# Attention beside a routed feed-forward: the lead of row maxima in groups of three pairs, V's last tile in another bank, one output tile finished by VectorE

## The chip, the cores and the metric

One core of a Trainium2 chip runs the whole program. Its engines work side by side, each through its own queue in program order: TensorE (PE, with the weight loads, PEld, as a second row of the profile), VectorE (DVE), ScalarE (ACT), GpSimd (POOL) and the queue of SyncE (SP), from which most DMAs are issued. They meet at semaphores. PE writes to PSUM, which has eight banks of 128 partitions x 512 float32; DVE and ACT read it, POOL doesn't. The metric is the device time of one execution in microseconds (us), the median of several; lower is better.

## The reference

x is 2048 x 512 (S x D), there are 32 heads of 16 columns, and everything is float32:

```python
g = sigmoid((x * gate_w).sum(-1, keepdims=True))
q, k, v = split_heads(x @ wqkv)
p = softmax(einsum("bhqd,bhkd->bhqk", q, k) * 16 ** -0.5)
a = merge_heads(einsum("bhqk,bhkd->bhqd", p, v)) @ wo
r = x @ w_r
idx = argsort(-r)[:, :2]
y = (silu(x[idx] @ w_gate) * (x[idx] @ w_up)) @ w_down * sigmoid(r[idx])
b = x + scatter_add(0, idx, y)
out = g * a + (1 - g) * b
```

## The kernel before

**Units.** Heads are taken two at a time (a pair of heads sits in rows 0 to 47 and 64 to 111 of `Qx` and `Kx`: high parts, low parts and a copy of 16 columns each). A pair of heads and one half of the queries is a unit; there are 32, and each has 16 steps, one for each 128 keys. Unit 0 uses `Kx[0]` and `Qx[0]`.

**What a unit needs first.** Softmax subtracts each row's maximum. `m_piece` and, ahead of the main loop, `m_lead` compute the scores with queries on the partitions (t: eight blocks of 128 queries; c: four blocks of 512 keys; j: the head of the pair) and reduce them on DVE to `Mr`, one column for each (t, c, j): 64 columns a unit (`EL`). `m_unit` takes the minimum over c of the negated maxima, `m_rows` transposes it and writes it by eight small DMAs on SP into rows 48 and 49 (and 112 and 113) of `Qx`, where it takes part in the second score matmul, `s_piece`. That one has the keys on the partitions; ACT takes its exp into `P`, and `av_mm` multiplies P with V (with a column of ones for the sums) into a bank that is collected over a unit's 16 steps.

**PSUM.** The eight banks have fixed names: `st` three in rotation, `mxa` two banks as one tile of 1024 columns, and one each of `mxb`, `av` and `fl`. A tile of a name waits until the engines have read what was in the same bank before (three allocations back for `st`, one for the others).

**The start.** Q and K of the first group of heads are projected, then comes the lead: `LEAD` = 21 steps, numbered -21 to -1. Each step calls `m_lead(n)`, which issues two pairs of matmuls (one pair into `mxa`, the second into two of `mxb`, `fl`, `av` in turn, both with the same t and neighbouring c) and three reductions on DVE; then three parts (four in the first step) of `lead_parts`; then the work filed for that step. A part is three matmuls on all 128 rows: the first four parts are the last projection of Q, the other 64 are V, four for each tile of 128 tokens (`v_part`). A V tile is collected in an `st` bank and copied to SBUF by ACT (L303) with its last part. 21 steps take 64 of the 68 parts; the last four, V's tile 15, are left to the main loop. `m_unit(0)` follows n = 15, `m_rows` of unit 0 n = 16.

**Work filed for steps** (`at_step`, run by `end_step`): `products(t)` at step -18 + t, two POOL multiplications of a block of x with w_r and gate_w; `sums(t)` at -17 + t, two ACT passes that add them up into `gz`; loads of x at -13 and -9; W of the second group of heads loaded at -8 and split at -5 (`split_w(1)`: high parts by ACT, low parts by POOL); `r_row` at -1, a PE transpose of `gz` into `fl`, copied by ACT when the main loop runs its list `late`. The products' tiles come from a ring of six, of which four are free for them, so products t wait for sums t - 2.

**The main loop** runs through the string `ORDER`, each letter of which issues one thing: `s` a score matmul with its exp, `m` one matmul of the maxima (with a reduction after the second and the third of each three), `A` P V of one step, `f` a filler (three matmuls of a later projection, in `fl`). The first two `A` come before P V has data: each takes two parts of V instead (L1025). The segments of the string are called rounds' segments below: "sssmmA", "smssmmA", "msssmmf", "smssmmA", and so on.

**The tail** (L796 to L848) multiplies the last unit's output with `wo` and stores the last output tiles of 128 tokens. A tile is brought to its end either by `finish`, one DVE instruction that reads PSUM, or by `acc_add`, an ACT copy with the gate's scale and a POOL addition. Tiles 10, 11, 12, 14 and 15 are finished by DVE, 9 and 13 by `acc_add`. The stores of 10, 11, 9, 12, 14 and 13 stand in this order on SP's queue; tile 15's two halves are stored from ACT's queue.

Of the kernel before, what the change touches and what calls it, by code (L numbers as in the profile page):

```python
# [21 lines left out]
KT = S // 128  # L22
VW = DH + 1
LEAD = 21
# [12 lines left out]
def gated_mix(ctx: ExitStack, tc: tile.TileContext, xT, x, wqkv, wo, w_rg, w_gate, w_up, w_down,  # L37
# [12 lines left out]
    def st_tile(shape=(128, 512)):  # L50
        return psum.tile(list(shape), F32, tag="st", name="st", bufs=3)
# [4 lines left out]
    def mxa_tile():  # L56
        return psum.tile([128, 2, 512], F32, tag="mxa", name="mxa", bufs=1)
# [4 lines left out]
    def av_tile():  # L62
        return psum.tile([128, 512], F32, tag="av", name="av", bufs=1)
# [229 lines left out]

    def v_part(t, c):
        if c == 0:
            VP[t] = st_tile()
        ps = VP[t]
        nb, tt = divmod(t, 4)
        sl = slice(tt * 128, tt * 128 + 128)
        for n, (a, b) in enumerate(((xh, wv[1]), (xl, wv[1]), (xh, wv[2]))):  # L300
            nc.tensor.matmul(ps, a[nb][:, c, sl], b[:, c, :], start=c == 0 and n == 0, stop=c == 3 and n == 2)  # L301
        if c == 3:
            nc.scalar.activation(Vh[:, t, :, :DH], ps.rearrange("p (h d) -> p h d", d=DH), AF.Copy)  # L303

    def lead_parts():

        v = [(t, c) for t in range(KT) for c in range(4)]
        yield from proj(0, "q", 3, 3)
        while v:
            v_part(*v.pop(0))  # L310
            yield


    rg = {}
# [27 lines left out]
    def r_row():  # L342
        ps = fl_tile((16, 128))
        nc.tensor.transpose(ps, gz[:, :, 0], ident)
        rg["row"] = ring.tile([16, 128], F32, tag="rt", name="rt", bufs=1)
        late.append((nc.scalar.activation, (rg["row"], ps, AF.Copy)))

    def route_rows():

# [124 lines left out]
    def acc_add(t, ps, scale):  # L474
        a = acc[t // 4][:, t % 4, :]
        w = o_tile("w", [128, D])
        nc.scalar.activation(w, ps, AF.Copy, scale=scale[:, t:t + 1])  # L477
        nc.gpsimd.tensor_add(a, a, w)  # L478
# [132 lines left out]

    def m_lead(n):

        if n < 16:
            u, t, c = 0, n // 8 * 4 + n % 4, n // 4 % 2 * 2
        else:
            u, t, c = 1, (n - 16) // 2, n % 2 * 2
        for i in range(3):
            if i == 0:
                tl = mxa_tile()  # L620
                dst = [tl[:, 0], tl[:, 1]]
            else:
                tl = (mxb_tile, fl_tile, av_tile)[(2 * n + i) % 3]()
                dst = [tl]
            for k, d in enumerate(dst):
                j, cc = (k, c) if i == 0 else (i - 1, c + 1)
                nc.tensor.matmul(d, Qx[u][64 * j:64 * j + 48, t * 128:t * 128 + 128],  # L627
                                 Kx[0][64 * j:64 * j + 48, cc * 512:cc * 512 + 512], start=True, stop=True)
            o = EL * u + t * 8 + (c * 2 if i == 0 else c * 2 + 1 + i)
            reds.append((Mr[:, o:o + len(dst)], tl))  # L630
        for r in reds:
            nc.vector.tensor_reduce(*r, axis=AX.X, op=OP.max, negate=True)  # L632
        reds.clear()
        if n == 15:
            m_unit(0)
        elif n == 16:
            m_rows(*turn.pop())

    reds = []
# [156 lines left out]
    def tail():  # L796
        u = UNITS - 1
        hl = [o_tile(n, [128, 512], F32R) for n in ("onh", "onl")]
        o = AV[u]
        ps = st_tile((128, 16))  # L800
        pw = mxa_tile()
        pw = pw[:, 0], pw[:, 1], st_tile()

        def late_wo(i):
            wo_terms(pw[i], *lastp[1], 3, slice((2 + i if i < 2 else 1) * 128, (3 + i if i < 2 else 2) * 128), True, True)

        late_wo(0)
        finish(10, pw[0])
        store(10)
        for c in range(4):  # L810
            nc.tensor.matmul(ps[:, 4 * c:4 * c + 4], o[:, c * 128:c * 128 + 128], sel_l, start=True, stop=True)
        r = ring.tile([128, 16], F32, tag="r16", name="rl", bufs=2)
        nc.vector.reciprocal(r, ps)
        rx = o_tile("rxl", [128, 16, 32])
        rb = r[:, :, None].to_broadcast([128, 16, 32])
        nc.scalar.activation(rx[:, 0:8], rb[:, 0:8], AF.Copy)
        nc.vector.tensor_copy(rx[:, 8:16], rb[:, 8:16])
        late_wo(1)
        finish(11, pw[1])
        store(11)  # L820
        pr = [mxb_tile((128, 256)), fl_tile((128, 256))]
        for c in range(4):
            nc.tensor.matmul(pr[c // 2][:, c % 2 * 128:c % 2 * 128 + 128],
                             rx[:, 4 * c:4 * c + 4].rearrange("p a b -> p (a b)"), ident, start=True, stop=True)
        for t in range(2):
            nc.vector.tensor_mul(o[:, 256 * t:256 * t + 256], o[:, 256 * t:256 * t + 256], pr[t])
        for t in range(2):
            sl = slice(256 * t, 256 * t + 256)
            split(hl[0][:, sl], hl[1][:, sl], o[:, sl])
        late_wo(2)  # L830
        acc_add(9, pw[2], gg)
        store(9)
        banks = [st_tile(), av_tile(), st_tile(), mxb_tile()]
        for t, n in ((0, 0), (0, 1), (1, 0), (1, 1), (0, 2), (1, 2), (2, 0), (2, 1), (2, 2), (3, 0), (3, 1), (3, 2)):
            a, b = ((0, 0), (0, 1), (1, 0))[n]
            nc.tensor.matmul(banks[t], hl[a][:, t * 128:t * 128 + 128], wz[0][:, b, :], start=n == 0, stop=n == 2)
            if n == 2 and t < 3:
                if t == 1:
                    acc_add(13, banks[t], gg)
                else:  # L840
                    finish(12 + t, banks[t])
                    store(12 + t)
        store(13)
        a = acc[3][:, 3, :]
        for i, eng in enumerate((nc.scalar, nc.scalar)):
            c = slice(256 * i, 256 * i + 256)
            nc.vector.scalar_tensor_tensor(a[:, c], banks[3][:, c], gg[:, 15:16], a[:, c], op0=OP.mult, op1=OP.add)
            eng.dma_start(out[15 * 128:, c], a[:, c])  # L848
# [4 lines left out]
    def at_step(s, f, *a):  # L853
        fill.setdefault(s, []).append((f, a))

    def end_step(s):
        now[0] = s
        for f, a in fill.pop(s, []):
            f(*a)
# [4 lines left out]
        at_step(-17 + t, sums, t)  # L864
    for t in range(16):
        at_step(-18 + t, products, t)
    at_step(-1, r_row)
    at_step(2, gaps.append, lambda: nc.vector.max(top8, rg["row"]))
    at_step(3, gaps.append, route_rows)
    at_step(1, gates, 0)  # L870
# [119 lines left out]
    def parts_next(n):  # L990
        for _ in range(n):
            next(parts, None)
# [4 lines left out]
            for c in (2 * nb - 4, 2 * nb - 3):  # L997
                split(wv[1][:, c], wv[2][:, c], wvs[:, c], lo_engine=nc.gpsimd)
    nc.sync.dma_start(cst, consts)
    for s in range(-LEAD, 0):  # L1000
        now[0] = s
        if s == -11:
            load_q(1)
        m_lead(s + LEAD)
        parts_next(3 + (s == -LEAD))
        end_step(s)
    count["m"] = 4 * LEAD

    while count["m"] < UNITS * EL:
# [71 lines left out]
```

## Time and profile before

| | us |
|---|---|
| median of 3 runs | 1415.55 (1415.53 to 1415.92) |
| the profiled execution | 1415.73 |
| its span, first to last instruction | 1413.8 |
| granted clock of TensorE | 1.000 |
| lead, first pair of maxima to the first score matmul of the main loop | 25.22 to 87.80 |
| last P V ends | 1401.4 |

The span is 1.93 us shorter than the execution's own time. A timeline row reads: start and duration in us, engine, line of the kernel, operation, output tile <- inputs, shapes, count, and in brackets how long the engine had been idle and what released it. A row of stretches reads: from and to, length, then the busy time of PE, PEld, DVE, ACT and POOL with their instruction counts, the granted clock, the share of time in which the DMA engines were busy, and GB/s. Durations of matmuls are modelled and overlap; starts are what to go by. Durations of DVE and ACT instructions overlap their neighbours by up to a tenth of a microsecond too.

### The profile page before, as it was taken

The numbers are of one execution on the slowest core, as the hardware profiler recorded it, in microseconds if no ns is written. First come the engines' busy times: TensorE is split into PE (matmuls) and PEld (weight loads), VectorE is DVE, ScalarE is ACT, GpSimd is POOL, SyncE is SP. The second block draws the span as 40 slices with busy tenths as digits, with TensorE's granted clock in tenths as the row PEclk, the third lists the DMA queues.
The fourth block names the chain that finished last, engine by engine and source line by source line (L and its number), as shares of the span: only waits on it lengthen the run. The fifth ranks groups of instructions, "written<-read, shape, count | busy, mean of one in ns | idle before, by whom it ended". The sixth has DMA issues, their size and how long they took to land.

```text
span 1413.8 us, 24075 instructions
## 1 busy us (share of the span) xinstructions
PE 1405.9 (99%) x9109; PEld 626.4 (44%) x9109; DVE 1287.5 (91%) x1535; ACT 1169.9 (83%) x2263; POOL 316.7 (22%) x335
## 2 busy tenths in 40 slices
PE   9999999999999999999999999999999999999998
PEld 6654444444444444444444443344444444444433
DVE  6889999999999999999999999999999999999943
ACT  5568888888888888888888888888888888888986
POOL 3841101102000001200000100043722322224411
PEclk9999999999999999999999999999999999999999
DMA  8712111312123221312222342424312121111002
GB/s 265 272 31 57 46 40 39 84 39 69 44 74 101 70 61 39 83 38 72 66 91 61 93 102 76 103 60 120 84 46 54 32 68 29 29 31 51 15 32 99
DMA packets 54775, 101.24 MB, mean 72 GB/s; under 512 B 13168, under 2 KB 20592, under 8 KB 53028
## 3 DMA queue, kind: packets, MB, share of 16 engines
q1 hardware_dynamic: 53796, 98.62, 24.6%
q8 instruction: 72, 1.18, 0.4%
q10 hardware_dynamic: 576, 0.79, 0.2%
q0 software_dynamic: 288, 0.30, 0.1%
q14 instruction: 43, 0.35, 0.1%
HBM read 63.77 MB, written 36.96 MB: 71 GB/s over the span
## 4 chain that ended last, share of the span: by engine, by line
PE 99%; DMA 0%; ACT 0%; DVE 0%; issue 0%; DVEq 0%
PE av L695 36%; PE st L672 23%; PE mxa L592 12%; PE mxb L592 10%; PE fl L155 6%; PE fl L511 4%; PE st L301 3%; PE st L155 2%; PE mxa L627 1%; PE fl L402 1%; PE mxa L672 0%; PE fl L440 0%; DMA ws<-wqkv 0%; PE mxa L511 0%; PE fl L627 0%; PE mxb L627 0%
## 5 line engine op out<-in xcount | busy, mean ns | idle before, releaser
L674 ACT ACTIVATE P<-st 128x512 f32<-128x512 f32 x2009 | 1055.3, 599 | 188.5 <-PE st L672 101.7
L596 DVE TENSOR_REDUCE Mr<-mxa 128x2 f32<-128x1024 f32 x655 | 796.1, 1215 | 2.6 <-PE mxa L592 2.5
L695 PE MATMUL av<-P,V 128*32 128x512 f32 x4096 | 545.6, 605 | 0.2 <-DVE o L704 0.2
L672 PE MATMUL st<-Qx,Kx 50*128 50x512 f32 x2009 | 531.4, 443 | 0.8 <-ACT P L674 0.6
L596 DVE TENSOR_REDUCE Mr<-mxb 128x1 f32<-128x512 f32 x654 | 451.0, 690 | 61.0 <-PE st L672 18.8
L672 PEld LDWEIGHTS st<-Qx,Kx 50*128 50x128 f32 x2009 | 276.5, 184 | 228.3 <-ACT P L674 208.7
L592 PE MATMUL mxb<-Kx,Qx 48*128 48x512 f32 x654 | 325.2, 497 | 0.0
L592 PE MATMUL mxa<-Kx,Qx 48*128 48x512 f32 x1310 | 294.1, 417 | 0.0
L592 PEld LDWEIGHTS mxb<-Kx,Qx 48*128 48x128 f32 x654 | 119.5, 183 | 273.7 <-DVE Mr L596 272.8
L695 PEld LDWEIGHTS av<-P,V 128*32 128x32 f32 x4096 | 81.1, 108 | 142.7 <-issue 135.9
L592 PEld LDWEIGHTS mxa<-Kx,Qx 48*128 48x128 f32 x1310 | 123.1, 183 | 44.3 <-DVE Mr L596 2.6
L208 POOL TENSOR_SCALAR ev<-pe 128x512 fp32r<-128x512 f32 x24 | 35.8, 1490 | 411.5 <-ACT pe L206 411.5
L478 POOL TENSOR_TENSOR acc<-acc,w 128x512 f32<-128x512 f32 x36 | 46.1, 1280 | 201.0 <-ACT w L477 200.9
L77 POOL TENSOR_SCALAR hl<-m 128x16 fp32r<-128x16 f32 x31 | 7.8, 253 | 296.5 <-DVE m L643 296.5
L155 PE MATMUL fl<-xh,wh 128*128 128x512 f32 x96 | 42.9, 447 | 0.0
L155 PE MATMUL fl<-xh,wl 128*128 128x512 f32 x96 | 40.5, 422 | 0.0
L511 PE MATMUL fl<-woh,ahl 128*128 128x512 f32 x96 | 35.1, 447 | 0.0
L562 DVE SCALAR_TENSOR_TENSOR acc<-fl,gg,acc 128x512 f32<-128x512 f32 x11 | 8.2, 747 | 28.8 <-PE fl L511 28.8
L632 DVE TENSOR_REDUCE Mr<-mxa 128x2 f32<-128x1024 f32 x21 | 25.7, 1222 | 8.5 <-PE mxa L627 8.5
L155 PE MATMUL fl<-xl,wh 128*128 128x512 f32 x96 | 32.6, 421 | 0.0
L303 ACT ACTIVATE V<-st 128x512 f32<-128x512 f32 x16 | 9.6, 600 | 27.5 <-PE st L301 27.5
L209 POOL TENSOR_TENSOR ev<-pe,ev 128x512 fp32r<-128x512 f32 x24 | 30.8, 1285 | 2.0
(192 smaller groups left out, 786.4 us busy)
## 6 DMA issues: line engine op xcount, KB each, us to landing
Kx<-k_scr SPq DMA_DIRECT2D x30, 384.0 KB
Qx<-q_scr SPq DMA_DIRECT2D x52, 192.0 KB
q_scr<-ev SPq DMA_DIRECT2D x15, 512.0 KB
k_scr<-ev SPq DMA_DIRECT2D x13, 512.0 KB
xn<-x SPq DMA_DIRECT2D x4, 1024.0 KB
Qx<-hr SPq DMA_DIRECT2D x256, 2.0 KB
acc<-x_scr SPq DMA_DIRECT2D x4, 1024.0 KB
q_scr<-ev SPq DMA_DIRECT2D x15, 256.0 KB
```

Source lines behind the costliest of these rows:

```text
L155: nc.tensor.matmul(ps, a[:, i, c, :], b[nb][:, c, :], start=n == 0, stop=n == 11)
L208: nc.gpsimd.tensor_scalar(ev[:, 0], t, 1.0, None, op0=OP.mult)
L209: nc.gpsimd.tensor_sub(ev[:, 1], t, ev[:, 0].bitcast(F32))
L301: nc.tensor.matmul(ps, a[nb][:, c, sl], b[:, c, :], start=c == 0 and n == 0, stop=c == 3 and n == 2)
L478: nc.gpsimd.tensor_add(a, a, w)
L511: nc.tensor.matmul(ps, a[:, sl], b[:a.shape[0], c, :], start=first and n == 0, stop=last and n == 2)
L592: nc.tensor.matmul(dst, Qx[u % 3][64 * j:64 * j + 48, t * 128:t * 128 + 128], k_of(u, t // 4)[64 * j:64 * j + 48, c * 512:c * 512 + 512], ...
L596: nc.vector.tensor_reduce(Mr[:, g0:g0 + (2 if r == 1 else 1)], MX[r - 1], axis=AX.X, op=OP.max, negate=True)
L632: nc.vector.tensor_reduce(*r, axis=AX.X, op=OP.max, negate=True)
L672: nc.tensor.matmul(ps, k, q, start=True, stop=True)
L674: nc.scalar.activation(P[s][:, 2 * j + c, :], ps, AF.Exp)
L695: nc.tensor.matmul(AV[0][32 * ct:32 * ct + 32, :], V[:, kt, h * VW:h * VW + 32], P[s][:, ct, :], start=kt == 0, stop=kt == KT - 1)
```

## The change

Three edits, with what follows from them:

1. `m_lead` runs 14 times and issues three pairs each time: the first into `mxa`, the second into an `st` and the `av` bank, the third into `mxb` and `fl`. A pair has one (t, c) and both heads. DVE reduces the double bank with one instruction and the other four banks with one each. After a group come five parts, or four in every third group (n = 1, 4, 7, 10, 13), 65 in all, and then the filed work of one or two steps, so that 14 groups cover the same 21 steps. `m_unit(0)` follows group 10, `m_rows` of unit 0 group 11, `load_q(1)` comes before group 6.
2. V's tile 15 is collected in the `av` bank. Its first part lies in the lead, the other three in the main loop. `r_row` is no longer filed for step -1: it is the last of the parts, right behind V's tile 15, and ACT's copy follows it at once rather than from the list `late`.
3. In the tail, tile 9 is brought to its end by `finish` (one DVE instruction), not by `acc_add` (ACT and POOL).

```diff
     def v_part(t, c):
         if c == 0:
-            VP[t] = st_tile()
+            VP[t] = av_tile() if t == KT - 1 else st_tile()
...
         while v:
             v_part(*v.pop(0))
             yield
+        r_row()
+        yield
...
-        late.append((nc.scalar.activation, (rg["row"], ps, AF.Copy)))
+        nc.scalar.activation(rg["row"], ps, AF.Copy)
...
     def m_lead(n):
 
-        if n < 16:
-            u, t, c = 0, n // 8 * 4 + n % 4, n // 4 % 2 * 2
-        else:
-            u, t, c = 1, (n - 16) // 2, n % 2 * 2
         for i in range(3):
+            p = 3 * n + i
+            if p < 32:
+                u, t, c = 0, p // 16 * 4 + p // 2 % 4, p // 8 % 2 * 2 + p % 2
+            else:
+                u, t, c = 1, (p - 32) // 4, p % 4
             if i == 0:
-                tl = mxa_tile()
-                dst = [tl[:, 0], tl[:, 1]]
+                tl = [mxa_tile()]
+                dst = [tl[0][:, 0], tl[0][:, 1]]
             else:
-                tl = (mxb_tile, fl_tile, av_tile)[(2 * n + i) % 3]()
-                dst = [tl]
-            for k, d in enumerate(dst):
-                j, cc = (k, c) if i == 0 else (i - 1, c + 1)
+                dst = tl = [st_tile(), av_tile()] if i == 1 else [mxb_tile(), fl_tile()]
+            for j, d in enumerate(dst):
                 nc.tensor.matmul(d, Qx[u][64 * j:64 * j + 48, t * 128:t * 128 + 128],
-                                 Kx[0][64 * j:64 * j + 48, cc * 512:cc * 512 + 512], start=True, stop=True)
-            o = EL * u + t * 8 + (c * 2 if i == 0 else c * 2 + 1 + i)
-            reds.append((Mr[:, o:o + len(dst)], tl))
+                                 Kx[0][64 * j:64 * j + 48, c * 512:c * 512 + 512], start=True, stop=True)
+            o = EL * u + t * 8 + c * 2
+            w = 2 // len(tl)
+            for j, k in enumerate(tl):
+                reds.append((Mr[:, o + j:o + j + w], k))
...
-        if n == 15:
+        if n == 10:
             m_unit(0)
-        elif n == 16:
+        elif n == 11:
             m_rows(*turn.pop())
...
         late_wo(2)
-        acc_add(9, pw[2], gg)
+        finish(9, pw[2])
         store(9)
...
-    at_step(-1, r_row)
...
-    for s in range(-LEAD, 0):
-        now[0] = s
-        if s == -11:
+    for n in range(LEAD * 2 // 3):
+        now[0] = n * 3 // 2 - LEAD
+        if n == 6:
             load_q(1)
-        m_lead(s + LEAD)
-        parts_next(3 + (s == -LEAD))
-        end_step(s)
+        m_lead(n)
+        parts_next(4 if n % 3 == 1 else 5)
+        for s in range(n * 3 // 2, (n + 1) * 3 // 2):
+            end_step(s - LEAD)
```

## The prediction

> **What bounds the kernel now.** I read the page, then the busy time of each engine in the lead, then the timelines of TensorE (PE), ScalarE (ACT), GpSimd (POOL) and VectorE (DVE) at the places that the diff touches: the lead (25 to 88 us), the first three rounds of the main loop, and the last 10 us. The page, and the lead's row (us; then busy us and instructions of each engine, granted clock, DMA share, GB/s):
>
> ```profile
> span 1413.8 us, 24075 instructions
> ...
> PE 1405.9 (99%) x9109; PEld 626.4 (44%) x9109; DVE 1287.5 (91%) x1535; ACT 1169.9 (83%) x2263; POOL 316.7 (22%) x335
> ...
> 25.00:91.00 66.00, 65.85 (x292) 42.88 (x291) 53.62 (x70) 32.82 (x87) 44.40 (x37) 1.00 0.56 187
> ```
>
> PE is the bound, in the lead too, so a change pays what it takes off PE's own sequence, plus what it takes off the end behind PE. "Busy" hides how densely PE works; that is read from start to start. One group of the lead (start, duration):
>
> ```profile
> 34.89 0.50 PE L627 MATMUL mxa<-Kx,Qx 48*128 48x512 f32 x2
> ...
> 35.23 0.39 PE L627 MATMUL av<-Kx,Qx 48*128 48x512 f32 x1
> ...
> 35.56 0.50 PE L301 MATMUL st<-Kx,xh 128*128 128x512 f32 x1
> 35.89 0.40 PE L301 MATMUL st<-Kx,xl 128*128 128x512 f32 x1
> ...
> 37.50 0.39 PE L301 MATMUL st<-wvl,xh 128*128 128x512 f32 x1
> ...
> 37.82 0.50 PE L627 MATMUL mxa<-Kx,Qx 48*128 48x512 f32 x2
> ```
>
> The two matmuls of a pair use different rows of the array and run side by side. Pair 1 to pair 2: 0.34 us. Pair 2 to the first V matmul: 0.33. First to second V: 0.33. Then V costs 0.23 each (35.89 to 37.50 in 7). Last V to the next pair: 0.32. A group of 2 pairs and 9 V matmuls is 2.93 us, of which 9 x 0.23 = 2.07 is V and 0.86 is pairs and the two changes of form.
>
> **The lead in threes.** The work stays: 42 pairs. What a third pair costs in a row isn't in the lead; the main loop has three 48- and 50-row pairs in a row, before P V:
>
> ```profile
> 98.38 0.74 PE L672 MATMUL st<-Qx,Kx 50*128 50x512 f32 x3
> ...
> 98.96 0.43 PE L592 MATMUL mxa<-Kx,Qx 48*128 48x512 f32 x2
> ...
> 99.32 1.07 PE L695 MATMUL av<-P,V 128*32 128x512 f32 x8
> ```
>
> From the first pair to the third 0.58 = 0.34 + 0.24. So I take 0.24 for the third (bounds: 0.23, a bare matmul, and 0.34, if it pays like the second). A new group with 5 parts (15 V matmuls) is 0.34 + 0.24 + 0.33 + 0.33 + 13 x 0.23 + 0.32 = 4.55, one with 4 parts 4.55 - 0.69 = 3.86. Nine and five of them: 60.25. Before, 21 x 2.93 + 0.69 for the extra part of the first, + 0.69 for the part that the new lead does more (65 for 64): 62.91. PE saves 2.66; the lower bound, with 0.34, is 14 x 0.10 less, 1.26.
>
> [...]
>
> Banks: per group one double and four single reductions. Their spacing at the lead's start, one first reduction from the middle, and the eight writes of unit 0's row of maxima on SP's queue:
>
> ```profile
> 27.38 1.21 DVE L632 TENSOR_REDUCE Mr<-mxa 128x2 f32<-128x1024 f32 x1
> 28.51 0.68 DVE L632 TENSOR_REDUCE Mr<-fl 128x1 f32<-128x512 f32 x1
> 29.11 0.68 DVE L632 TENSOR_REDUCE Mr<-av 128x1 f32<-128x512 f32 x1
> ...
> 35.43 1.22 DVE L632 TENSOR_REDUCE Mr<-mxa 128x2 f32<-128x1024 f32 x1 [0.39 <-PE mxa L627]
> ...
> 76.15 5.39 SPq L663 DMA_DIRECT2D Qx<-hr  x8
> ```
>
> Start to start 1.13 and 0.60: 1.13 + 4 x 0.60 = 3.53 a group, 14 x 3.53 = 49.4 in all against 21 x 2.33 = 48.9 before; the 0.5 more lies beside PE. The first starts 0.54 after its pair (35.43 - 34.89), so fl, the last, is read by 0.54 + 1.13 + 3 x 0.60 + 0.68 = 4.15 after the group's start; the next group wants it at 3.86 + 0.58 = 4.44 at the earliest. The cover is 0.29, and there is no wait in steady state. At the start there is one: DVE's first reduction comes at 27.38 as before, as it stands behind Q's eviction, so fl is free at 27.38 + 1.13 + 1.80 + 0.68 and an estimated 0.06 for the signal = 31.05, while the second group (25.22 + 4.55 = 29.77; 25.22 is the lead's start) wants it at 30.35: 0.70, and 0.09 for a fresh weight load. The third waits 0.17 + 0.09. Total 1.05. The lead's st bank waits for a V eviction further up the rotation; the tightest I found, in group 8, wants it at 60.93 where V's tile 7 leaves at 60.67: no wait. So group 3 starts at 39.22, 5 at 47.63, 11 at 73.55, 12 at 78.10, 13 at 82.65, and the main loop at 25.22 + 60.25 + 1.05 = 86.5. The row's writes follow group 11's reductions: issued from 78.2 to 83.6, with S at 86.5; SP's other loads keep their order.
>
> **The gates' sums in ACT's order.** Now two steps' sums can come behind two V evictions. This is what may be late next:
>
> ```profile
> 53.09 0.62 ACT L332 ACTIVATE p<-p 128x512 f32<-128x512 f32 x1
> ...
> 53.88 1.29 POOL L328 TENSOR_TENSOR p<-xn,wr 128x512 f32<-128x512 f32 x1 [0.34 <-ACT p L332]
> ...
> 76.55 0.62 ACT L332 ACTIVATE p<-p 128x512 f32<-128x512 f32 x1
> ...
> 77.78 1.14 ACT L70 ACTIVATE wh<-ws 128x512 fp32r<-128x512 f32 x2
> ...
> 78.47 2.55 POOL L71 TENSOR_TENSOR wl<-ws,wh 128x512 fp32r<-128x512 f32 x2 [2.21 <-ACT wh L70]
> ...
> 80.12 0.39 PE L301 MATMUL st<-wvl,xh 128*128 128x512 f32 x1
> ...
> 80.97 1.29 POOL L328 TENSOR_TENSOR p<-xn,wr 128x512 f32<-128x512 f32 x1
> ...
> 80.55 0.60 ACT L303 ACTIVATE V<-st 128x512 f32<-128x512 f32 x1 [0.40 <-PE st L301]
> ```
>
> Products t wait for sums t-2, 0.79 after those start; a pair of sums takes 1.23; W's low half starts 0.69 after ACT's split and takes 2.50; products take twice 1.29 and overlap by 0.08, so 2.50; a V eviction starts 0.43 after its last matmul's start, so 0.91 + 0.10 - 0.23 + 0.43 = 1.21 after the group's start plus 0.69 for each part up to it, and ACT goes on 0.5 later. In group 5 sums 3 stand behind the eviction of V's tile 5, 47.63 + 1.21 + 5 x 0.69 = 52.29, so products 5 can't start before 52.79 + 0.79 = 53.58. In group 11 sums 12 and the split of W stand behind V's tile 12: 78.21; sums 12 at 78.71, split at 79.94, W's low half at 80.63, products 14 at 83.13 and 15 at 85.62, ready at 88.20. Sums 15, which stand ahead of every exp of the main loop, end at 88.8, 2.3 after the main loop begins. Before, the exps began 0.64 after it (88.44 against 87.80, below).
>
> **The first three rounds.** Before:
>
> ```profile
> 87.59 0.27 PE L344 MATMUL fl<-cst,gz 128*16 128x128 f32 x1
> ...
> 87.80 1.15 PE L672 MATMUL st<-Qx,Kx 50*128 50x512 f32 x3
> ...
> 89.11 0.50 PE L301 MATMUL st<-Kx,xh 128*128 128x512 f32 x1
> ...
> 90.70 0.50 PE L672 MATMUL st<-Qx,Kx 50*128 50x512 f32 x1
> ...
> 91.89 0.50 PE L672 MATMUL st<-Qx,Kx 50*128 50x512 f32 x1 [0.44 <-ACT P L674]
> ...
> 94.14 1.25 PE L672 MATMUL st<-Qx,Kx 50*128 50x512 f32 x3
> ...
> 96.45 0.49 PE L672 MATMUL st<-Qx,Kx 50*128 50x512 f32 x1
> ...
> 88.44 1.52 ACT L674 ACTIVATE P<-st 128x512 f32<-128x512 f32 x3
> ```
>
> From the first S to the first round with P V (96.45) 8.65 us; V's last tile held one of three st banks there. Moving it to av frees S of that wait. After: S0 at 86.5; V's tile 14 leaves after sums 14 at 86.9, so S1 goes at 87.0. Exps at 88.8 with 0.48 between them release S3 at 89.47, S4 at 89.95, S5 at 90.43. Then m, m (0.66), V's last three matmuls and the row transpose (1.1): third segment at 92.2; its three pairs (0.91) and three fill matmuls (0.33 + 0.23 + 0.32) make the fourth 94.0, that is 2.45 earlier than before. ACT's eviction of V and copy of the row fall behind S5's exp and end near 92.9, ahead of the fill's fl at 93.1. av waits for nothing: P V comes at 95. The moved transpose costs the same 0.21 and no longer needs sums 15 ahead of S. From here to the tail PE's sequence is the same, and at 99% busy it carries the 2.45 through.
>
> **The tail.** Tile 9 goes from ACT and POOL to one DVE instruction:
>
> ```profile
> 1405.76 0.76 DVE L71 TENSOR_TENSOR onl<-o,onh 128x256 fp32r<-128x256 f32 x2 [0.16 <-ACT onh L70]
> ...
> 1406.72 1.30 POOL L478 TENSOR_TENSOR acc<-acc,w 128x512 f32<-128x512 f32 x1 [19.17 <-ACT w L477]
> ...
> 1407.24 0.75 DVE L562 SCALAR_TENSOR_TENSOR acc<-st,gg,acc 128x512 f32<-128x512 f32 x1 [0.72 <-PE st L836]
> ...
> 1408.05 0.81 SPq L565 DMA_DIRECT2D out<-acc  x2
> ...
> 1408.95 0.92 SPq L565 DMA_DIRECT2D out<-acc  x2
> ...
> 1409.00:1409.50 0.50, 0.00 (x0) 0.00 (x0) 0.50 (x2) 0.00 (x0) 0.50 (x1) 1.00 1.04 393
> ...
> 1411.50:1412.00 0.50, 0.00 (x0) 0.00 (x0) 0.00 (x0) 0.00 (x0) 0.00 (x0) 1.00 1.01 375
> ```
>
> DVE is free at 1406.52 for 0.72, the new instruction takes 0.75 and overlaps its neighbour by 0.06: no delay for tile 12. Tile 9 is done at 1407.25, not 1408.02, and its store, queued ahead of the others on SP, is issued at 1407.3. The last stores keep all DMA engines full (share 1.0) from 1409 to 1412 at some 380 GB/s: with 128 x 512 x 4 bytes sent ahead, 0.69 us less is left for that stretch, if nothing runs dry; tile 14's store is issued only at 1408.95, so I take off 0.2 for a gap before it and count 0.5 (bounds 0 and 0.69).
>
> **Sum.** 2.45 + 0.5 = 2.95. The profiled execution took 1415.73 (span 1413.8 and 1.93 around it): 1412.78; the median of the runs lies 0.18 under it: **1412.6**. Faster by more than 0.2% (2.83 us, about what a measurement of this kernel can tell from no change) begins at 1412.72, so the forecast lies close to that line.
>
> **Rivals.**
> - The third pair pays 0.34. Twelve groups before the chain of sums make it 12 x 0.10 later: about 1413.8. For: pair 2 pays it. Against: 98.96.
> - PE doesn't feel the late sums. If the exps start when S does, the three rounds cost their bare PE time, 0.91 + 1.59 (89.11 to 90.70), 0.91 + 1.1, and 1.79, 6.3 from 86.5: 92.8, 1.2 earlier: 1411.4. For: ACT is busy half the lead, so products can catch up. Against: the split of W behind tile 12.
> - DVE becomes the lead's bound. If reductions don't overlap (1.22 + 4 x 0.68 = 3.94), fl is free at 4.54, 0.10 late after each of the five shorter groups, with 0.09 for a fresh load 0.95 in all, and the two waits at the start grow by 0.8: 1414.35; the eight writes slip by as much and have the room. For: DVE is at 53.62 of 66.00. Against: 29.11 follows 28.51 by 0.60.
> - Slower: the sums' chain grows. Place: ACT's order in groups 5, 7, 9, 11, where products wait behind V evictions. Every microsecond by which sums 15 end after 88.8 stops S outright, as all three st banks are full. From 2.95 later (91.75) the change loses; were two more groups to hold POOL for a V tile's four parts (4 x 0.69 = 2.76) each, the time is 1412.6 + 5.5 = 1418.1. Against: products 6 to 13 need only 2.5 each and groups last 3.9 or more.
>
> **Chances.** Forecast 0.50 (its own range 1412.0 to 1413.5, somewhat over half on the faster side), third pair 0.19, no late exps 0.15, DVE 0.08, slower 0.08. Faster: 0.30 + 0.15 + a little of the rest = 0.47; within 0.2%: 0.45; slower 0.08. The range takes in the unknown costs (0.34 for the third pair, no gain at the tail) and the earlier exps: 1411.2 to 1414.9.
>
> **What would show it.** Right: the lead's groups 4.5 and 3.9 apart; the third pair 0.24 behind the second; one stall near 30.5; sums 15 ending near 88.8 with S3 to S5 waiting for exps; the fourth segment 2.45 earlier; store 9 at about 0.75 less before the end, and the drain 0.5 shorter. Wrong: groups at 4.65 and more, DVE without idle time in the lead, PE idle over 1 us after the lead, or a changed distance from the first P V to the tail.

## The result and the profile after

The changed kernel takes 1412.22 us (median of 9 runs, 1410.94 to 1413.86) against 1415.55 of the kernel before (9 runs beside it): a ratio of 0.9977, with a 95% interval of 0.9969 to 0.9985. It is faster by 3.3 us, 0.23%; the interval reaches to both sides of the 0.2% line. 1412.6 was predicted, with a range of 1411.2 to 1414.9. The profiled execution is the fastest of the nine, 1410.94. The page of after, its first lines, and then its row of stretches for the lead:

```profile
span 1409.2 us, 24079 instructions
...
PE 1402.5 (100%) x9109; PEld 628.4 (45%) x9109; DVE 1289.3 (91%) x1543; ACT 1168.8 (83%) x2262; POOL 315.9 (22%) x334
```

```profile
25.00:91.00 66.00, 66.00 (x302) 45.62 (x300) 55.70 (x79) 34.28 (x89) 44.65 (x37) 1.00 0.58 192
```

These rows hardly differ from those of before: the busy shares can't show the change. The starts do. PE's timeline of after, the first pairs of groups 4 and 5 of the lead with group 4's other pairs (groups count from 0), group 12's last pair, the first rounds of the main loop (S stands for a score matmul there, P V for a multiplication with V), and the last P V:

```profile
43.02 0.50 PE L628 MATMUL mxa<-Kx,Qx 48*128 48x512 f32 x2
43.36 0.39 PE L628 MATMUL st<-Kx,Qx 48*128 48x512 f32 x1
...
43.59 0.39 PE L628 MATMUL mxb<-Kx,Qx 48*128 48x512 f32 x1
...
43.92 0.50 PE L301 MATMUL st<-Kx,xh 128*128 128x512 f32 x1
...
46.86 0.50 PE L628 MATMUL mxa<-Kx,Qx 48*128 48x512 f32 x2
...
77.69 0.39 PE L628 MATMUL mxb<-Kx,Qx 48*128 48x512 f32 x1
78.01 0.50 PE L628 MATMUL fl<-Kx,Qx 48*128 48x512 f32 x1
...
85.97 0.73 PE L675 MATMUL st<-Qx,Kx 50*128 50x512 f32 x3
...
88.48 0.49 PE L675 MATMUL st<-Qx,Kx 50*128 50x512 f32 x1
...
92.91 0.50 PE L675 MATMUL st<-Qx,Kx 50*128 50x512 f32 x1
...
94.10 1.07 PE L698 MATMUL av<-P,V 128*32 128x512 f32 x8
...
1394.17 3.05 PE L698 MATMUL av<-P,V 128*32 128x512 f32 x24
```

A group of four parts is 46.86 - 43.02 = 3.84 long (3.86 predicted), and the third pair comes 0.23 behind the second (0.24 predicted). The fourth segment of S stands at 92.91, where before had it at 96.45: 3.54 earlier, not 2.45. The same points in before, P V's first and last start in PE's timeline:

```profile
97.38 1.07 PE L695 MATMUL av<-P,V 128*32 128x512 f32 x8
...
1398.31 3.05 PE L695 MATMUL av<-P,V 128*32 128x512 f32 x24
```

By stages of the profiled executions (the lead starts at 25.22 before and at 25.32 after; the table's numbers are differences of unrounded starts, so a rounded row can be 0.01 off):

| us | before | after | gain |
|---|---|---|---|
| start of the lead to the first S | 62.58 | 60.66 | 1.92 |
| first S to first P V | 9.59 | 8.12 | 1.47 |
| first P V to the last (one program) | 1300.92 | 1300.07 | 0.85 |
| last P V to the end | 15.51 | 15.00 | 0.51 |

The third row isn't the change's: its instructions are the same, and over the twelve profiles of this study in which the clock held there it lies between 1299.9 and 1301.8; in runs 10 and 11 below it came to some 1300.0 and 1301.5 (the span less the first P V's start and a tail of 15.0). What sets it was not found. The prediction named a changed length of this stage as a sign that it is wrong; with a spread of 1.9 in unchanged instructions that sign can't be used. So totals of single executions are good to some 2 us, and what follows is read from the stages and from medians of kernels run together on one chip.

The tail, ACT, DVE's two multiplications of accumulators and POOL in one timeline of after:

```profile
1402.29 1.55 DVE L564 SCALAR_TENSOR_TENSOR acc<-st,gg,acc 128x512 f32<-128x512 f32 x2
...
1403.33 0.69 ACT L479 ACTIVATE w<-av,gg 128x512 f32<-128x512 f32 x1 [1.42 <-PE av L839]
...
1404.09 1.28 POOL L480 TENSOR_TENSOR acc<-acc,w 128x512 f32<-128x512 f32 x1 [20.69 <-ACT w L479]
```

DVE now finishes two tiles in a row, 1.55 us, and POOL's only addition is tile 13's. Tile 9's store is issued 8.89 us after the last P V's start, 9.74 before: 0.85 earlier, where some 0.75 was predicted. The DMA engines, nearly full in before from 1409 to 1412 (a share of 0.97 to 1.04 in each half microsecond), are busy for 0.77, 0.82 and 0.76 of the half microseconds from 1404.5 to 1406 here, so part of that is lost in gaps, as the prediction allowed for. What is left is 0.51, for the predicted 0.5.

### The profile page after: what moved, and what is told of

Its sections match the earlier page's. It is cut to its first block, busy times and chain, and to the rows that moved or that the text cites. A ratio compares the mean times of both kernels' runs of the same rounds, so it can differ in the third digit from the quotient of the medians.

```text
span 1409.2 us, 24079 instructions
## 1 busy us (share of the span) xinstructions
PE 1402.5 (100%) x9109; PEld 628.4 (45%) x9109; DVE 1289.3 (91%) x1543; ACT 1168.8 (83%) x2262; POOL 315.9 (22%) x334
## 4 chain that ended last, share of the span: by engine, by line
PE 99%; DMA 0%; DVE 0%; ACT 0%; DVEq 0%; issue 0%
PE av L698 36%; PE st L675 23%; PE mxa L594 12%; PE mxb L594 10%; PE fl L155 6%; PE fl L513 4%; PE st L301 3%; PE st L155 2%; PE fl L404 1%; PE mxa L628 0%; PE mxa L675 0%; PE fl L442 0%; DMA ws<-wqkv 0%; PE av L301 0%; PE st L628 0%; PE mxb L628 0%
## 5 line engine op out<-in xcount | busy, mean ns | idle before, releaser
L598 DVE TENSOR_REDUCE Mr<-mxa 128x2 f32<-128x1024 f32 x655 | 796.5, 1216 | 1.4 <-PE mxa L594 1.3
L474 POOL TENSOR_SCALAR acc<-acc,omg 128x512 f32<-128x512 f32 x16 | 24.9, 1569 | 11.0 <-PE st L675 11.0
```

Of the source, the lines that this page charges most:

```text
L474: nc.gpsimd.tensor_scalar(a, a, omg[:, t:t + 1], None, op0=OP.mult)
L598: nc.vector.tensor_reduce(Mr[:, g0:g0 + (2 if r == 1 else 1)], MX[r - 1], axis=AX.X, op=OP.max, negate=True)
```

## The experiments

Each kernel was timed with runs of the kernel before on its chip. Runs 1 to 4 were made together, one after the other on one chip (before: 1415.12), and so were 5 to 8 (1416.57) and 9 to 12 (1415.03); only runs of one set are compared by their times.

**1. The changed kernel again**, unedited.

> The changed kernel as it stands. By my reading the gain has three places: the first S of the main loop and the three segments behind it (the fourth segment begins 3.3 us earlier than before), the tail (0.5 shorter), and nothing in between. So 3.3 to 3.9 us under the kernel before, and the same distances in a second trace: groups of the lead 4.5 and 3.85 apart, sums 15 ending about 1.9 us after the first S. Rival: the profile that I have seen was an exceptional execution, in which Q's eviction at 25.4 did not wait for a DMA; where it waits (26.1 before), the second group stalls 0.7 and the gain falls to about 2.5.

Measured: 1411.80 (11 runs), ratio 0.9977 (0.9968 to 0.9986). Its stages: 61.68 to the first S, 8.12, 1299.94, 15.00. The lead was 1.02 longer than in the first profile of the same program. ACT's timeline, first of after, then of this run:

```profile
25.43 0.60 ACT L73 ACTIVATE ev<-st 128x512 fp32r<-128x512 f32 x1 [2.12 <-PE st L155]
...
87.84 3.02 ACT L677 ACTIVATE P<-st 128x512 f32<-128x512 f32 x6
```

```profile
26.43 0.60 ACT L73 ACTIVATE ev<-st 128x512 fp32r<-128x512 f32 x1 [3.16 <-DMA k_scr<-ev]
...
88.84 3.02 ACT L677 ACTIVATE P<-st 128x512 f32<-128x512 f32 x6
```

And PE's timeline of this run:

```profile
30.73 0.50 PE L628 MATMUL mxb<-Kx,Qx 48*128 48x512 f32 x1
31.33 0.50 PE L628 MATMUL fl<-Kx,Qx 48*128 48x512 f32 x1
...
86.97 0.73 PE L675 MATMUL st<-Qx,Kx 50*128 50x512 f32 x3
...
93.90 0.50 PE L675 MATMUL st<-Qx,Kx 50*128 50x512 f32 x1
```

The profiles show two kinds of executions. Where Q's eviction (L73) waits for a store, the whole start is 1 us late: the second group (group 1) stalls for its banks, the exps begin at 88.84 and the fourth segment at 93.90. The profile of before shows that wait too (26.14), and the prediction's stalls rest on it. Of the eleven profiles with the lead in threes, three have the late eviction (runs 1, 5 and 6). The old lead hardly felt it: 62.58 to the first S with the wait, 62.41 without (run 2).

**2. Before with the tail alone.**

```diff
-        acc_add(9, pw[2], gg)
+        finish(9, pw[2])
```

> The kernel before with tile 9 alone finished by VectorE. My theory: store 9 goes out about 0.75 us earlier and the drain of the stores ends 0.45 earlier; 0.4 to 0.6 us under the kernel before, last P V to the end 15.0 instead of 15.5. Rival (a transfer that is hidden anyway): tile 13's store sets the end, no change within 0.1.

Measured: 1414.44, ratio 0.9997 (0.9988 to 1.0006); last P V to the end 15.02 for before's 15.51. By the median it is 0.7 faster than before, by the stage 0.49. The total alone can't be told from no change; the stage can.

**3. Before with V's last tile in av**, the row transpose behind it, and five parts in the first step of the old lead.

```diff
-            VP[t] = st_tile()
+            VP[t] = av_tile() if t == KT - 1 else st_tile()
...
+        r_row()
+        yield
...
-    at_step(-1, r_row)
...
-        parts_next(3 + (s == -LEAD))
+        parts_next(3 + 2 * (s == -LEAD))
```

> The kernel before with V's last tile in the av bank, the row transpose behind it, and one part of V more in the lead; the lead stays in groups of two pairs. My theory: the first S comes 0.5 later (one more part, no transpose), the three segments then cost their bare 6.3 instead of 8.65, as the sums are done before S here: the fourth segment 1.85 earlier, total 1.6 to 2.1 under before. Rival: the waits of S come from ACT's rate and not from the bank that V holds; then the segments still cost about 8 and the gain is under 0.5.

Measured: 1413.79, ratio 0.9990 (0.9981 to 0.9999): 1.3 faster. The first S comes later, 63.34 after the lead's start, as one more part stands there; then the first P V follows it by 7.43, where before needs 9.59. ACT's timeline shows why that is less than the 8.12 of after:

```profile
89.34 1.58 ACT L676 ACTIVATE P<-st 128x512 f32<-128x512 f32 x3 [0.88 <-PE st L674]
```

The exps begin 0.53 after the first S (88.81) and wait for PE, not for sums. The expected 1.6 to 2.1 is missed all the same: from the first S to the fourth segment it needs 6.24, as expected (6.3), but the first S comes 0.76 later than in before, not 0.5.

**4. Before with the lead in threes alone**; V's last tile stays in st and the transpose at step -1 (the diff's `m_lead` and its loop, nothing else).

> The kernel before with the lead in 14 groups of three pairs alone: V's last tile in an st bank, the row transpose filed for the last step, the tail as before. My theory: the groups are 4.5 and 3.85 apart, but the transpose of the gates' sums now waits on TensorE for sums 15, which end near 87.9: about 1.8 us of idle TensorE at the lead's end, and the waits of S for the bank of V's tile stay. About 1 us under before (0.5 to 1.5) of the 2.7 that the groups save. Rival: the three edits add up; then this is 2.5 or more under before.

Measured: 1415.63 (1414.54 to 1422.03), ratio 1.0010 (0.9998 to 1.0021); the median shows none of the gain that was expected. The profiled execution took 1419.78. PE's timeline, and then the stretches of 3.41 us:

```profile
86.90 0.28 PE L344 MATMUL fl<-cst,gz 128*16 128x128 f32 x1 [0.79 <-ACT p L332]
...
88.76 0.49 PE L673 MATMUL st<-Qx,Kx 50*128 50x512 f32 x1 [0.92 <-ACT P L675]
...
90.61 0.63 PE L301 MATMUL st<-Kx,xl 128*128 128x512 f32 x1
91.04 0.63 PE L301 MATMUL st<-wvl,xh 128*128 128x512 f32 x1
```

```profile
86.78:90.19 3.41, 2.38 (x9) 1.42 (x10) 0.66 (x1) 2.50 (x7) 0.53 (x1) 1.00 0.51 135
90.19:93.60 3.41, 3.15 (x9) 1.62 (x8) 1.26 (x2) 1.08 (x2) 0.00 (x0) 0.51 0.00 0
...
103.84:107.25 3.41, 3.41 (x28) 1.02 (x25) 3.18 (x4) 2.90 (x6) 0.00 (x0) 0.99 0.00 0
```

At its old place the transpose stands ahead of S and needs the last sums, so the lead's gain is waited away (0.79), then S waits for exps (0.92). After that idle time the granted clock falls to one half (the third number from the end: 1.00, 0.51, 0.99), matmuls go 0.43 apart instead of 0.23, and only after 13.65 us, at 103.84, does it come back. The first P V is at 100.87. Executions differ in this. Six of the eleven runs have a mean granted clock of 1.000 and lie between 1414.54 and 1415.63, five of them 0.3 to 0.6 under before; the other five have 0.999 to 0.993 and lie between 1416.11 and 1422.03, longer the lower the clock. So the lead in threes alone gains at most some 0.6 where the clock holds, at the lower end of the expected 0.5 to 1.5, and loses where it falls, which the expectation didn't have. By the medians the three edits, alone, make 0.7 + 1.3 - 0.5 = 1.5, and with 0.6 for the lead 2.6; together they make 3.3. The lead's gain comes through in full only with the second edit.

**5. The changed kernel with V's last tile back in st**, the transpose still behind it.

```diff
-            VP[t] = av_tile() if t == KT - 1 else st_tile()
+            VP[t] = st_tile()
```

> The changed kernel with V's last tile back in an st bank; lead, late row transpose and tail stay. It parts the bank from the moved transpose. My theory: the moved transpose is what lets the lead's gain through (without it TensorE stood idle and its granted clock fell to 0.50), so no idle time at the lead's end and no lowered clock here; the bank is worth the waits of S for it, about 1 us: first S as in the changed kernel, first P V 1 us later, 0.7 to 1.3 us slower than the changed kernel (2.0 to 2.6 under before). Rival: bank and transpose do the same job and either is enough: no slower than the changed kernel.

Measured: 1418.69 (1415.01 to 1422.72), ratio 1.0013 (1.0003 to 1.0023). PE's timeline and the stretches:

```profile
89.36 0.50 PE L675 MATMUL st<-Qx,Kx 50*128 50x512 f32 x1 [1.99 <-ACT P L677]
```

```profile
87.12:90.53 3.41, 1.42 (x7) 0.78 (x6) 0.41 (x1) 2.77 (x7) 0.94 (x1) 1.00 0.56 153
90.53:93.94 3.41, 3.15 (x10) 1.52 (x9) 1.46 (x2) 0.67 (x2) 0.00 (x0) 0.50 0.00 0
```

The wait for a bank was expected, at 0.7 to 1.3; it is 1.99, and its real price is the clock behind it: from the first S to the first P V 14.93. In other executions the clock falls less or not at all (1415.01 to 1416.19 at 0.999 or 1.000, the rest at 0.998 to 0.994), but even the fastest is 1.7 over the 1413.3 that the changed kernel's ratio of 0.9977 gives in this set. So moving the transpose isn't enough; the bank is needed as well. The bank moved without the transpose was not run.

**6. The changed kernel with unit 0's low part of the maxima set to 0**, in place of its subtraction. DVE's timeline of after has a row that the prediction didn't foresee; the same row of before stands in the second block, and POOL's timeline of after in the third:

```profile
73.21 1.22 DVE L651 TENSOR_TENSOR hl<-m,hl 128x16 fp32r<-128x16 f32 x1
74.35 1.21 DVE L635 TENSOR_REDUCE Mr<-mxa 128x2 f32<-128x1024 f32 x1
```

```profile
73.46 0.18 DVE L648 TENSOR_TENSOR hl<-m,hl 128x16 fp32r<-128x16 f32 x1
```

```profile
73.12 1.28 POOL L330 TENSOR_TENSOR p<-xn,wr 128x512 f32<-128x512 f32 x1
74.36 1.29 POOL L330 TENSOR_TENSOR p<-xn,wg 128x512 f32<-128x512 f32 x1
```

16 columns take 1.22 us where they took 0.18, and end when POOL's multiplication ends (74.43 and 74.40), although the next multiplication follows without a gap. Group 12's fl (78.01 above) stalls behind it by 0.32, and the matmul behind fl comes another 0.10 late (0.43 after it for the usual 0.32), so that the group is 4.95 long for the 4.52 of others of its size.

```diff
-            nc.vector.tensor_sub(hl[:, :, 1], m, hl[:, :, 0].bitcast(F32))
+            nc.vector.memset(hl[:, :, 1].bitcast(F32), 0.0)
```

> The changed kernel, with the low part of unit 0's maxima set to 0 instead of computed by VectorE (softmax is shifted by the high part alone). In the changed kernel this 128x16 subtraction took 1.22 us where it began under a GpSimd multiplication, 0.18 before, where GpSimd was idle; fl came late for group 12's third pair by 0.3. My theory: both read two tensors from SBUF and VectorE waits until GpSimd's instruction is through; a memset reads none and takes 0.2 or less; group 12's wait is gone, first S 0.3 to 0.4 earlier, 0.1 to 0.4 us faster than the changed kernel. Rival: the time is that of the chain of three small VectorE instructions, each waiting for the one before; then the memset takes about as long and nothing changes.

Measured: 1413.26, ratio 0.9977 (0.9967 to 0.9987), the changed kernel's own ratio. The stall is gone (lead 61.09 with the late Q eviction, for run 1's 61.68), but the first S to the first P V takes 8.57 for 8.12, and the fourth segment is at 93.90 in both. What PE saves in the lead it waits for in the first rounds. The subtraction was what held DVE, as expected; the 0.1 to 0.4 us that this was to gain didn't come.

**7. The changed kernel with the late sums earlier**: products and sums of blocks 8 to 15 and the split of W one step sooner.

```diff
-        at_step(-17 + t, sums, t)
+        at_step(-17 + t - (t > 7), sums, t)
...
-        at_step(-18 + t, products, t)
+        at_step(-18 + t - (t > 7), products, t)
...
-    at_step(-5, split_w, 1)
+    at_step(-6, split_w, 1)
```

> The changed kernel with sums and products of blocks 8 to 15 one step earlier and W's split one step earlier, ahead of V's tiles 11 and 12 in ScalarE's order. My theory: the exps of the main loop begin some 1.9 us after the first S only because sums 15 stand ahead of them; here sums 15 end before V's tile 14 is evicted, the exps begin 0.6 after the first S, S to first P V costs 7.43 as with the lead in twos instead of 8.12: 0.5 to 0.9 us faster than the changed kernel. Rival: TensorE hides the late sums already (it has V's last tile to do), no change within 0.2.

Measured: 1421.81, ratio 1.0036 (1.0023 to 1.0049): slower than before by 5.2. From the first S to the first P V it needs the expected 7.44, but the lead takes 70.62. The timelines of DVE, POOL and PE:

```profile
73.46 8.45 DVE L651 TENSOR_TENSOR hl<-m,hl 128x16 fp32r<-128x16 f32 x1
81.84 1.21 DVE L635 TENSOR_REDUCE Mr<-mxa 128x2 f32<-128x1024 f32 x1
```

```profile
80.61 1.27 POOL L330 TENSOR_TENSOR p<-xn,wr 128x512 f32<-128x512 f32 x1
81.96 1.26 POOL L330 TENSOR_TENSOR p<-xn,wg 128x512 f32<-128x512 f32 x1
```

```profile
83.11 0.80 PE L628 MATMUL mxa<-Kx,Qx 48*128 48x512 f32 x2 [5.66 <-DVE Mr L635]
```

The same subtraction now stands on DVE for 8.45 us. POOL works from one multiplication into the next without a gap until 81.88 (80.61 + 1.27); in the first 0.08 us in which it rests, the subtraction ends (81.91). All reductions queue behind it, PE idles 5.66 us, and the granted clock is 0.50 for 10.24 us, from 81.26 to 91.50. That the subtraction, not POOL's work as such, was the cause was a theory at this point; runs 10 and 11 try it.

**8. The changed kernel with the stores of the first K and Q tiles issued earlier**, so that Q's eviction never waits for them.

```diff
-        if (which, nb) in (("k", 1), ("q", 2), ("q", 3)):
+        if (which, nb) in (("q", 0), ("q", 2), ("q", 3)):
...
-            for e in scr[:2] if nb == 1 else scr:
+            for e in scr:
```

> The changed kernel with the stores of K and Q of the first 512 tokens issued before the second block of K, 3 us earlier on SP's queue. My theory: the spread of the changed kernel (1410.9 to 1413.9) and its distance from its fastest come from Q's third eviction, which in some executions waits for the DMA that empties its buffer (26.4 instead of 25.4); the second group then stalls 1 us. Here it never waits: first S 60.7 after the lead's start in each, median 0.5 to 0.9 under the changed kernel and a narrower spread. Rival: the spread has another source, median and spread stay.

Measured: 1415.82, ratio 0.9994 (0.9985 to 1.0002), 2.5 us more than the changed kernel's ratio of 0.9977 would make it. Q's eviction came early (25.64), but SP's queue now holds rows of K behind the stores, and PE waits for them:

```profile
28.69 0.47 PE L628 MATMUL st<-Kx,Qx 48*128 48x512 f32 x1 [2.65 <-DMA Kx<-evx]
```

Behind this wait the granted clock is one half (0.50) for 3.40 us, from 29.30 to 32.70, and the lead takes 64.94. By the runs' clocks this too differs between executions: 1413.79 to 1414.62 with 1.000, up to 1417.85 with 0.997. The expectation missed that with the stores issued earlier on SP's queue its neighbours there came later (PE's wait of 2.65).

**9. The changed kernel beside the last three**, unedited.

> The changed kernel once more, beside the next three on one chip, so that they are compared with it and not only with the kernel before. Expected ratio to the kernel before 0.9977, the two earlier measurements' value, within 0.001. Its profile should again have the high-low subtraction of unit 0 on VectorE at about 73.2 to 74.2 us lasting 1.2 us while GpSimd multiplies (0.18 us in the kernel before, where GpSimd stood idle), group 12's stall of 0.3 to 0.4 us behind it, and from the first S to the first P V 8.1 us. The main loop (first P V to last) came out between 1299.9 and 1302.6 us in the runs so far, with the same program: if it differs again from chip to chip, differences between kernels of under 1 us are only read from the lead's stages of the profiles, or from the medians on one chip.

Measured: 1411.44 (1411.07 to 1412.96, 8 runs), ratio 0.9974 (0.9964 to 0.9985). Lead 60.66, then 8.14; the subtraction lasts 1.22.

**10. Runs 6 and 7 together**: sums early, unit 0's low part 0.

> The earlier sums once more (products and sums of blocks 8 to 15 and the weights' split one step earlier), with unit 0's low part set to 0 by a fill in place of VectorE's two-input subtraction. Theory: with the earlier sums alone the subtraction stood on VectorE for 8.45 us, from 73.46, exactly until GpSimd's unbroken work ended, and all reductions queued behind it; without it VectorE waits for nothing of GpSimd. Then the lead takes 60.2 to 61.2 us from its start to the first S, first S to first P V 7.4 us, the granted clock stays at 1.0, and the time is 0.7 to 1.3 us under the changed kernel on this chip. Rival: GpSimd's unbroken work itself slows VectorE or ScalarE (the one-input reductions too): then the reductions are late again, PE idles 5 us before group 13, the clock falls to 0.5 and the time is 8 us over the changed kernel. Second rival: the sums' start is not what holds the first rounds: S to P V stays at 8.1 and the time equals the changed kernel's.

Measured: 1410.78 (1409.92 to 1413.15, 9 runs), ratio 0.9971 (0.9961 to 0.9981), 0.66 under run 9. Lead 60.18, then 7.43, and in the profile the clock stays at 1.00; the slowest run, 1413.15, has 0.998. DVE's timeline at the subtraction's place:

```profile
73.24 0.07 DVE L651 MEMSET hl<- 128x16 f32 x1
73.25 1.23 DVE L635 TENSOR_REDUCE Mr<-mxa 128x2 f32<-128x1024 f32 x1
```

POOL works as densely as in run 7 and no reduction is late. So it was the two-input subtraction alone that was held.

**11. The same with the whole computation**: the subtraction is POOL's own.

```diff
-            nc.vector.tensor_sub(hl[:, :, 1], m, hl[:, :, 0].bitcast(F32))
+            nc.gpsimd.tensor_sub(hl[:, :, 1], m, hl[:, :, 0].bitcast(F32))
```

> The earlier sums with the whole computation kept: unit 0's subtraction is GpSimd's, between two of its products, in place of VectorE's. Theory: as with the fill, VectorE never waits for GpSimd; GpSimd pays one small subtraction (0.1 to 0.4 us) and, if it reaches it before VectorE's two minima at 73.2 to 73.9, a wait of up to 1 us, which the wait for the sums in step 0 hides or shows as up to 0.5 us. So lead to first S 60.2 to 61.2 us, first S to first P V 7.4 to 8.0, time 0.3 to 1.3 us under the changed kernel. Rival: GpSimd, in order, waits for VectorE's reductions, and the products and sums behind it become late: first S to first P V over 8.1 and the time at or over the changed kernel's.

Measured: 1410.68 (1409.86 to 1411.44, 6 runs), ratio to before 0.9968 (0.9955 to 0.9980): 0.76 under the changed kernel in that set, though the two sets of runs overlap between 1411.07 and 1411.44. The stages say it more sharply: from the lead's start to the first P V 67.67 us for run 9's 68.80. Timelines of POOL, ACT and PE:

```profile
73.25 0.22 POOL L651 TENSOR_TENSOR hl<-m,hl 128x16 fp32r<-128x16 f32 x1 [0.26 <-DVE hl L650]
```

```profile
86.07 1.58 ACT L677 ACTIVATE P<-st 128x512 f32<-128x512 f32 x3 [0.58 <-PE st L675]
```

```profile
91.79 0.50 PE L675 MATMUL st<-Qx,Kx 50*128 50x512 f32 x1
...
92.97 1.06 PE L698 MATMUL av<-P,V 128*32 128x512 f32 x8
```

On POOL the subtraction costs 0.22 and a wait of 0.26. The exps wait for PE again, not for sums. Nothing of the computation is left out, and no other kernel has a lower ratio.

**12. The changed kernel with the subtraction on POOL**, sums as they were.

> The changed kernel with that one subtraction on GpSimd and nothing else. Theory: group 12's stall of 0.3 to 0.4 us is gone from the lead, but the fourth segment of S is set by the sums of block 15 on ScalarE and not by the lead, as with the fill alone (93.90 us with and without the stall), so the time equals the changed kernel's within 0.3 us. Rival: the lead sets the end, and the time falls by 0.4 us; or GpSimd's products become late behind the subtraction and it rises by up to 0.5 us.

Measured: 1411.27 (1411.09 to 1411.59, 8 runs), 0.17 from run 9. The lead takes 60.19, 0.47 less than run 9's, and the first S to the first P V 8.57, 0.43 more. The stall was hidden by the wait for the sums.

## Why the prediction came out right

**The groups and the third pair: right.** 60.25 was predicted for the lead without stalls. Runs 10, 11 and 12, with neither Q's wait nor the held subtraction, took 60.18, 60.23 and 60.19. That the numbers are so close is in part luck: groups are 4.52 and 3.84 long, not 4.55 and 3.86, which makes 0.4 less in 14 of them, and these runs still hold 0.3 of stalls in groups 1 and 2. The third pair came 0.23 to 0.24 behind the second wherever the bank was free, so the rival at 0.34 (1413.8) is out: the third pair's matmuls follow the second's, on the same rows of the array, no later than one bare matmul follows another (0.23).

**DVE's cover: right, and the rival that it becomes the lead's bound is out,** as the bare 60.2 has no room for it: in after DVE is idle for 0.22 us before the reductions of groups 5 and 8, which follow a short group, and for 0.88 to 1.16 before those of seven others. What the working left out is one instruction of DVE's, the subtraction for unit 0. It was taken at its old 0.18 us, because before's trace has it at a moment at which POOL rested; the new lead moved it under a multiplication, where it took 1.22. The cover of 0.29 was too small for that, and group 12 lost 0.43. The prediction has no term for it; by run 12 it cost the end nothing.

**The stalls at the start: right for one kind of execution.** Predicted were 0.79 in group 1 and 0.26 in group 2, 1.05 in all. With the late Q eviction (run 1) these groups are 1.11 and 0.24 longer than others of their size, 1.35 in all, as the eviction stood 1.15 us after the lead's start there and 0.92 in the profile of before. Without it (after) they are 0.03 and 0.28 longer. So the working took a wait from a single profile as if it were always there, and for the kind of execution that has it the stalls came out 0.3 too short. The 0.4 that the groups were counted too long makes up for that: group 11 starts at 73.60 in run 1, for 73.55, and group 12 at 78.11, for 78.10. That the two errors cancel is luck.

**The late sums: right.** The exps were to begin at 88.8 and did at 88.84 in run 1; the fourth segment was to start at 94.0 and did at 93.90. The chain to the exps runs as it was told, with the starts in run 1 and the predicted ones in brackets: sums 12 at 78.71 (78.71), the split of W at 79.94 (79.94), its low half at 80.64 (80.63), products 14 at 83.14 (83.13). It also absorbs the miss in the lead: the first S came at 86.97, not at 86.5, but what follows waits for the exps. In after the exps and the fourth segment are both 1 us earlier, because in that execution Q's eviction was. Runs 3, 10 and 11, in which sums come in time, need 7.4 from the first S to the first P V instead of 8.1, so the wait for sums is worth 0.7 behind a lead that has the subtraction's stall; behind one without it, 1.1 (8.57 in run 12, 7.43 in run 10). The rival without late exps (6.3 from S to the fourth segment) is what run 10 shows: 85.64 to 91.86, 6.22. The changed kernel wasn't that case, but could be made so.

**The slower side.** The rival had sums so late that S stops. Its mechanism exists, only at another place than named: in runs 4 and 5 S stopped for the transpose and for a bank, and in the profiled executions most of the price wasn't the microseconds of the wait but the clock behind it (run 4: waits of 0.79 and 0.92, and 13.76 from the first S to the first P V for before's 9.59; run 5: a wait of 1.99, and 14.93 for after's 8.12). The prediction had no such term. With the bank moved and the transpose behind V none of the changed kernel's three profiles lists a wait of PE there; S merely follows the exps' pace.

**The tail: right.** 0.51 and 0.49 (run 2) for 0.5, with tile 9's store issued 0.85 earlier and some of that lost in the drain.

**The sum.** Predicted 2.95. By the stages that the change touches: 1.92 + 1.47 + 0.51 = 3.90 without Q's wait (after's profile) and 0.90 + 1.47 + 0.51 = 2.88 with it (run 1). The medians of three sets show gains of 3.3, 3.3 and 3.6, between these two. So 2.95 was the sum for the kind with the wait. That the medians lie higher because they mix both kinds is not shown: the main loop's own spread of 1.9 is larger than the difference of the kinds, and of the changed kernel's three profiled executions the slowest (1412.96, run 9) is one without the wait.

## What to carry to other kernels

Stages that hand work to each other don't add up edit by edit: the lead in threes alone was 0.5 us slower by the median, with the clock lowered in five of its eleven runs, and with the bank and the transpose moved it carried the gain. So an edit that fails alone is to be tried with its companions before it is judged. When a schedule is compressed, look at what an instruction newly runs beside, not only at what it waits for: one small VectorE instruction with two SBUF inputs cost 0.18 (before), 1.22 (after) or 8.45 us (run 7), depending on what GpSimd did at the time. And before a stall seen in one profile is counted, look in a second one whether it is always there.

## What the runs showed of the hardware

**A held VectorE instruction.** Run 7's subtraction ended only when GpSimd rested (8.45 us from 73.46, to 81.91, 0.03 after GpSimd's last), while one-input reductions and the fill of run 10 beside equally dense GpSimd work were not slowed: the fill 0.07, the reductions 0.68 and 1.23 as elsewhere. In after the subtraction began 0.09 after a multiplication of GpSimd's and ended 0.03 after it, 1.22 us in all. Why the one waits for the other no run shows, nor how long it can last. In four profiles (after and runs 1, 4 and 9) the subtraction got through after that one multiplication, in 1.21 to 1.22 us, though GpSimd went on with the next without a gap; in run 7 it was passed over by the following six GpSimd instructions. What differs there is not known.

**The clock.** It fell to one half at these places, each read from rows of stretches:

| run | PE busy in the row before the fall, us | PE busy in the rows at one half, us | clock at one half |
|---|---|---|---|
| 4 | 2.38 of 3.41 | 13.39 of 13.65 | 90.19 to 103.84 |
| 5 | 1.42 of 3.41 | 13.41 of 13.67 | 90.53 to 104.20 |
| 7 | 0.14 of 4.00 | 8.39 of 10.24 | 81.26 to 91.50 |
| 8 | 0.85 of 3.50 | 3.40 of 3.40 | 29.30 to 32.70 |

The lengths are close to four, four, three and one times run 8's 3.40. In run 4 PE was busy for 70% of the row before the fall, in run 7 for 4%. In run 8 the clock was back after 3.40 us with PE busy throughout, while in runs 4 and 5 PE was busy for 3.15 us of the first 3.41 and for all of the 10.24 and 10.26 that followed before the clock came back. What decides the fall and the return was not settled here.
